# Attention beside a state-space convolution: key bounds moved behind the value transposes, three shift-row buffers, and a redrawn table of 32 stages

## The chip, the cores and the metric

The kernel runs on one core of a Trainium2 chip. Time is the device time of one execution in microseconds (us); for the kernel before it is the median of three runs. TensorE does the matmuls (PE in the profile; PEld is its loading of weights), VectorE is DVE, ScalarE is ACT, GpSimd is POOL and SyncE is SP. SP and POOL issue most of the DMAs. Each engine works through its own instructions in a fixed order; semaphores hold an instruction until what it needs is there.

## The reference

Two independent branches, whose outputs are put side by side:

```python
# A: a diagonal state-space convolution over L = 2048, D = 576, N = 128
K = einsum("dn,dnl,dn->dl", C, exp(dt * A * l), dt * B).real
y = irfft(rfft(pad(K)) * rfft(pad(u)))[:L] + u * Dskip
# B: attention with 32 query heads of 18 columns and one key and value head, S = 2048
q = (x @ wq) split into 32 heads;  k = x @ wk;  v = x @ wv
o = softmax(q @ k.T * 18 ** -0.5) @ v
b = concat(o) @ wo
```

## The kernel before, in words

**Attention** goes through the queries in four chunks of 512 columns, each chunk in 16 pairs of heads, each pair through 16 blocks of 128 keys. One turn for one pair of heads and one key block is called an exponential here, after its largest instruction: two score matmuls (`scores`, line 550, tile s) write a 128x1024 tile in one of three banks of PSUM, ScalarE takes the exponential of it (line 561; line 559 for the first 32, which have a bias) into one of ten P tiles, and TensorE multiplies two such tiles with the values (`product`, line 869, tile ops). There are 1024 exponentials, handled three at a time in `main`. Row 18 of the values is one, so the product also gives the softmax's denominators.

**Fillers** are everything else that TensorE does: query projections (`qproj`, tile q), output projections (`outproj`, tile op), and for the convolution the generation of its kernel (tile kg) and its transforms (hu, lu, hk, lk, iy). They share one bank of PSUM, got by `bank`, and each must be evacuated by VectorE before the next can begin. VectorE also computes the convolution's tables (tab, fr, sum, tt) and its products (acc, pt, us, ks).

**Where the order comes from.** The order of TensorE, VectorE and ScalarE is written out when the kernel is built. A planner, the class `Clock`, holds a planned time of each engine, and `main` puts fillers between scores and products by credits, planned waiting times and constants. `PLAN` sets those constants anew for each stage; a stage is 64 exponentials long (`self.step // 32`, since a step is two exponentials). The functions of the fillers are generators that yield what they wait for: `"v"` and a planned time for VectorE work, `"p"` for TensorE work.

**Key bounds.** The exponential has no running maximum; instead each head gets a bound from the largest absolute values of queries and keys. `settle`, called after the first three exponentials are issued, transposes the values (line 378, tile vp, in the fillers' bank) and copies them to v_sb. `bounds`, called after the third group of three, spreads the keys' maxima by six small matmuls (line 401, tile kmx, also in the fillers' bank) and reduces them to kmax (line 153). No query projection after the first may start before it.

**Shift rows.** After a query projection, `queries` stores its halves qh and ql to a DRAM tile qd through POOL's DMA queue, and `bound` computes the bound of its heads: a small matmul (tile up), a reduction (un), and a row sh (line 145) that POOL's queue writes into qd (line 530). The tile sh has one buffer. SP's queue then fetches the operands (aug) from qd.

**Normalizing.** When the products of a chunk are through, `normalize` loads the denominators, takes their reciprocals, stores them to DRAM (rden), loads them back spread over partitions (db, line 600, two buffers), and multiplies them into the heads' tile oT. The planner lets 4.6 planned us pass from the issue of the load to the multiplication. The output projections of the chunk follow.

**The convolution's sines.** Three times in the loop the convolution needs new powers: ScalarE then loads another table, takes two wide sines (lines 1182, 1184), and loads the table of the exponential again.

**The end.** `finish` divides the last group's products with two reciprocals of 128x256 (lines 701 and 714) and does the partial output projections that are left over (`self.rest`).

Of the kernel before, what the change touches and what calls it, by code (L numbers as in the profile page):

```python
# [9 lines left out]
F32 = mybir.dt.float32  # L10
F16 = mybir.dt.float16
# [6 lines left out]
P = 128  # L18
# [6 lines left out]
CT = 512  # L25
# [17 lines left out]
NS = 3  # L43
# [3 lines left out]
RATE = 1.84  # L47
PACE = 1.79
AHEAD = 0.7
TOTAL = 340.0  # L50
LAST = 576.841

GAP = 0.4
PLAN = {
    0: dict(RATE=1.86, PACE=1.856, AHEAD=0.729, TOTAL=340.0, GAP=0.359, DEFER=0.395, SLACK=3.285, HEAD=17.08, LEFT=1.086, C1=0.549, C2=0.718, C3=0.83, C4=1.39, C5=0.739, C6=1.059, C7=0.572, C8=0.186, C9=0.382, C10=0.431, C11=24.516, C12=11.926),
    1: dict(RATE=1.838, AHEAD=0.731, HEAD=10.76, C3=0.633, C4=1.288, C6=0.962, C8=0.227, C11=22.979),
    2: dict(AHEAD=0.937, TOTAL=426.375, SLACK=2.955, HEAD=8.992, LEFT=1.137, C3=0.83, C4=1.267, C6=0.825, C11=24.516),
    3: dict(AHEAD=0.729, TOTAL=340.0, DEFER=0.389, SLACK=3.285, HEAD=13.454, LEFT=1.086, C2=0.563, C6=1.059, C8=0.186),
    4: dict(PACE=1.877, DEFER=0.395, C2=0.718, C3=0.886, C8=0.257, C12=9.229),
    5: dict(DEFER=0.334, C1=0.507, C3=0.973, C9=0.468, C10=0.418),  # L60
    6: dict(C3=0.912, C4=1.331, C5=0.562, C8=0.216, C9=0.573, C12=11.451),
    7: dict(TOTAL=393.142, HEAD=15.028, C1=0.596),
    8: dict(PACE=1.856, C8=0.186, C12=14.796),
    9: dict(GAP=0.311, DEFER=0.395, C1=0.601, C2=0.561, C6=0.861, C9=0.468),
    10: dict(PACE=1.834, HEAD=14.988, C1=0.497, C9=0.382),
    12: dict(TOTAL=300.519, C1=0.607, C2=0.687, C12=11.271),
    13: dict(AHEAD=0.591, TOTAL=393.142, SLACK=2.63, C1=0.65, C5=0.726, C6=1.059, C10=0.39, C12=14.796),
    14: dict(C1=0.533, C2=0.561, C7=0.595, C9=0.379, C12=11.755),
    15: dict(AHEAD=0.503, C3=1.026, C4=1.582, C8=0.194),
}  # L70
# [143 lines left out]
class Attention:  # L214
# [36 lines left out]
    def setup(self, tp, conv):  # L251
# [5 lines left out]
        nc, cp, a, V = self.nc, self.cp, self.a, self.V  # L257
# [42 lines left out]
        self.outs, self.step, self.due, self.scaled = [], 0, 1 << 30, {}  # L300
        self.o_left = self.q_left = self.units = 0
        self.todo, self.busy, self.group = [], False, 0
        self.tails = []
        self.side_work = Stream(self.side(), self.k, 99.0)
        conv.begin(6)
        p1, small = (self.ps_s.tile([P, 2, CT], F32, tag="s", name=n) for n in ("first", "small"))
# [64 lines left out]
    def settle(self, conv):  # L371

        nc, V, K = self.nc, self.V, self.k
        km, ab, spread = self.km, self.ab0, self.spread
        h2, l2 = self.parts[2:]
        vp = self.bank(CT, "vp").rearrange("p (j n) -> p j n", j=4)
        for j in range(4):
            nc.tensor.transpose(vp[:, j, :], self.vt[:, j * P:(j + 1) * P], self.ident)
        for src, dst in ((ab[96:, 0:1], ab[96:, 1:2]), (km[96:, 4:5], ab[96:, 0:1]), (ab[96:, 1:2], km[96:, 4:5])):
            V.tensor_copy(dst, src)  # L380
        V.tensor_scalar(km[:, 0:4], spread[:, 136:140], km[:, 4:5], None, op0=ALU.mult)
        V.tensor_copy(self.v[:, :, :DH].rearrange("p (c j) d -> p c j d", j=4), vp.rearrange("p j (c d) -> p c j d", c=4)[:, :, :, :DH])
        for m in range(2, 5):
            if m < 4:
                self.place(m, h2, l2, 32 * m - 32, (nc.sync, nc.sync))
            V.memset(self.wq[m][0:1, 0, 0:1], 0.0)
            self.load_wq(m)
        conv.start()
        K.t += 1.0
        K.v = K.t + 2.0  # L390
        K.fill = K.v

    def bounds(self):

        nc, V, K = self.nc, self.V, self.k
        km, spread = self.km, self.spread
        self.bounded = True
        pk = self.bank(20, "kmx")
        for m in range(5):
            for b, n in ((0, 128),) if m < 4 else ((0, 64), (64, 64)):  # L400
                nc.tensor.matmul(pk[b:b + n, 4 * m:4 * m + 4], spread[:, 2 * m:2 * m + n], km[:, 0:4], start=True, stop=True, tile_position=(0, b))
        V.tensor_reduce(self.kmax, pk.rearrange("p (m c) -> p m c", c=4), axis=AX.X, op=ALU.max)
        V.tensor_scalar(self.kmax, self.kmax, FLOOR, 1.002, op0=ALU.max, op1=ALU.mult)
        K.pe(1.5)
        K.v = max(K.v, K.t + 0.5)
        K.fill = K.v + 0.25

    def load_wo(self):
        self.nc.vector.memset(self.wo[0:1, :, 0:1], 0.0)
# [86 lines left out]
    def bound(self, c, m, ab, n0, qd):  # L496

        nc, V, K = self.nc, self.V, self.k
# [73 lines left out]
    def normalize(self, c, ms):  # L572

        nc, V, K = self.nc, self.V, self.k
        od = self.od[c].rearrange("(h r) n -> h r n", r=32)
        if c < NCH - 1:
            oT = self.oT = self.cp.tile([P, 5, CT], F32, tag="oT", name=f"oT{c}")
            o = [oT[:, m, :] for m in range(5)]
        else:
            o = self.heads  # L580
# [13 lines left out]
        tiles, fetched = {}, {}  # L594
# [210 lines left out]
    def main(self, conv, flag):  # L805
        nc, K = self.nc, self.k
# [74 lines left out]
        for r in range(0, len(pairs), NS):  # L881
            new = range(r, min(r + NS, len(pairs)))
            self.step = new[-1] // 2
            globals().update(PLAN.get(self.step // 32, {}))
            ss = {}
            for i in new:
                c, g, kb, j = pairs[i]
                if (g, kb, j) == (0, 0, 0):
                    self.od[c] = self.dr.tile([8 * P, CT], F32, tag="od", name=f"od{c}")
                force(lambda: 16 * c + 2 * g + j in self.ready)  # L890
                ss[i] = self.scores(i, c, 2 * g + j, kb, 0.34 if i == r else 0.216)
            K.t += 0.12
            for i in new:

                while (i - NP) // 2 >= behind:
# [2 lines left out]
                c, g, kb, j = pairs[i]  # L898
# [27 lines left out]
            c, g, kb, j = pairs[new[-1]]  # L926
# [706 lines left out]
```

## Time and profile before

| | us |
|---|---|
| runs | 1140.82, 1141.29, 1143.82 |
| median | 1141.29 |
| the profiled execution's own time | 1140.67 |
| its span | 1138.9 |
| TensorE busy | 1080.4 |
| ScalarE busy | 998.9 |
| VectorE busy | 992.7 |

A row of the timeline has start, duration, engine, line, operation, the tile written, an arrow and the tiles read, and in brackets how long the engine was idle before it and what ended that. A row of waits has who waited for whom, the sum in us, how often, and the longest. A row of a stretch has its ends and length, then the busy time of PE, PEld, DVE, ACT and POOL (instructions in parentheses), the granted clock of TensorE as a share of full speed, the DMAs' share, and GB/s. TensorE's counts are passes: a matmul of 32-bit floats takes two.

### The profile page before, as it was taken

To read this page: it belongs to the slowest core of one execution; us is meant where nothing else is said; L and a number is where in the kernel's file an instruction comes from. 1 tells how busy PE (TensorE), PEld (TensorE's weight loads), DVE (VectorE), ACT (ScalarE), POOL (GpSimd) and SP (SyncE) were. 2 spreads that over 40 slices of the span, in tenths; PEclk is the share of its full clock that TensorE was granted. 3 is DMA by queue.
4 is the path that set the end of the run, shared out by engine and by line. 5 is a ranking of instruction groups with operands and counts; after the bars stand their busy time and mean duration, and the time that the engine had idled before them with its cause. 6 is when DMAs were issued, how large, how long until landed. Compare 5 with 4: busy or idle time off the path is not lost.

```text
span 1138.9 us, 33011 instructions
## 1 busy us (share of the span) xinstructions
PE 1080.4 (95%) x13886; PEld 395.6 (35%) x13886; DVE 992.7 (87%) x1692; ACT 998.9 (88%) x1052; POOL 140.0 (12%) x257
## 2 busy tenths in 40 slices
PE   6999999998998999999999999999989999999997
PEld 2333333333333333323333333333322333433423
DVE  3878998899899898998799899899699799799794
ACT  2878988888997899999898999899999999889993
POOL 4442324122023000000201211000000000000000
PEclk9999999999999999999999999999999999999999
DMA  7432234212222301122202301201222311311201
GB/s 224 146 101 75 64 118 135 63 39 50 84 82 87 95 29 59 50 88 88 89 9 82 106 22 36 97 29 40 68 95 67 99 40 38 97 39 35 72 30 59
DMA packets 59279, 83.37 MB, mean 73 GB/s; under 512 B 14867, under 2 KB 35335, under 8 KB 58613
## 3 DMA queue, kind: packets, MB, share of 16 engines
q1 hardware_dynamic: 47557, 73.24, 20.1%
q0 software_dynamic: 10848, 7.37, 2.6%
q8 instruction: 111, 1.82, 0.7%
q10 hardware_dynamic: 720, 0.58, 0.2%
q14 instruction: 43, 0.35, 0.1%
HBM read 46.59 MB, written 33.85 MB: 71 GB/s over the span
## 4 chain that ended last, share of the span: by engine, by line
PE 59%; DVE 21%; ACT 10%; issue 6%; DMA 3%; POOL 1%; DVEq 0%; SPq 0%; ACTq 0%
PE ops L869 24%; PE s L550 15%; ACT P L561 9%; PE op L211 5%; DVE tab L137 5%; PE kg L1314 3%; DVE ks L137 3%; PE iy L211 3%; PE q L427 2%; DVE acc L137 2%; DVE tt L137 1%; PE hu L211 1%; PE hk L211 1%; DVE pt L137 1%; DMA db<-rden 1%
## 5 line engine op out<-in xcount | busy, mean ns | idle before, releaser
L561 ACT ACTIVATE P<-s 128x1024 f32<-128x1024 f32 x992 | 934.8, 1035 | 97.2 <-PE s L550 94.3
L869 PE MATMUL ops<-P,v_sb 128*32 128x512 f32 x4096 | 509.5, 599 | 3.0 <-DVE o L141 2.8
L550 PE MATMUL s<-aug,kaug 55*128 55x512 f16 x2048 | 307.5, 381 | 23.6 <-ACT P L561 20.8
L550 PEld LDWEIGHTS <-kaug 55*128 55x128 f16 x2048 | 93.2, 94 | 341.6 <-issue 292.9
L869 PEld LDWEIGHTS ops<-P,v_sb 128*32 128x32 f32 x4096 | 118.2, 110 | 162.8 <-issue 131.0
L478 POOL DMA_DIRECT2D qd<-qh x116 | 66.3, 578 | 317.8 <-DVE qh L145 315.2
L427 PE MATMUL q<-x,wq_sb 128*32 128x256 f32 x1360 | 83.6, 382 | 0.3 <-PE s L550 0.3
L211 PE MATMUL op<-wo_sb,oT 126*32 126x288 f32 (+1 forms) x960 | 67.5, 410 | 2.5 <-DVE ob L141 2.5
L1225 POOL MEMSET fr<- 128x192 f32 x24 | 9.9, 497 | 481.6 <-DVE tt L137 242.5
L137 DVE TENSOR_TENSOR tab<-tab,tt 128x576 f32<-128x576 f32 (+1 forms) x72 | 59.0, 820 | 1.5
L137 DVE TENSOR_TENSOR tab<-fr,dif 128x576 f32<-128x576 f32 (+1 forms) x72 | 58.7, 815 | 0.0
L137 DVE TENSOR_TENSOR tt<-fr,sum 128x576 f32<-128x576 f32 (+1 forms) x72 | 58.7, 815 | 0.0
L137 DVE TENSOR_TENSOR tab<-sum,fr 128x576 f32<-128x576 f32 (+1 forms) x72 | 58.6, 814 | 0.0
L137 DVE TENSOR_TENSOR tab<-tab 128x576 f32<-128x576 f32 (+1 forms) x72 | 58.5, 813 | 0.0
L141 DVE COPY ksb<-kg 128x192 f32<-128x192 f32 x48 | 17.3, 360 | 41.5 <-PE kg L1314 41.5
L427 PEld LDWEIGHTS q<-x,wq_sb 128*32 128x32 f32 x1360 | 39.9, 109 | 38.4 <-issue 14.4
L137 DVE TENSOR_TENSOR acc<-acc,pt 128x1728 f32<-128x1728 f32 (+2 forms) x36 | 48.6, 1349 | 0.2
L137 DVE TENSOR_TENSOR pt<-us,ks 128x1728 f32<-128x1728 f32 (+2 forms) x36 | 48.3, 1347 | 0.0
L1314 PE MATMUL kg<-tab 128*32 128x64 f32 x2304 | 41.8, 220 | 5.6 <-DVE tab L137 3.4
L1314 PEld LDWEIGHTS kg<-tab 128*32 128x32 f32 x2304 | 36.5, 110 | 29.6 <-issue 9.8
L559 ACT ACTIVATE P<-s,bias 128x1024 f32<-128x1024 f32 x32 | 33.0, 1115 | 13.4 <-PE s L550 13.4
L137 DVE TENSOR_TENSOR ks<-ks 128x576 f32<-128x576 f32 (+1 forms) x48 | 41.0, 855 | 1.0
(163 smaller groups left out, 1020.9 us busy)
## 6 DMA issues: line engine op xcount, KB each, us to landing
od<-o SPq DMA_DIRECT2D x31, 256.0 KB
aug<-qd SPq DMA_DIRECT2D x124, 55.0 KB
u<-u SPq DMA_DIRECT2D x12, 384.0 KB
kd<-ksb SPq DMA_DIRECT2D x12, 384.0 KB
kt<-kd SPq DMA_DIRECT2D x48, 96.0 KB
outa<-u SPq DMA_DIRECT2D x12, 384.0 KB
pw<-pw SPq DMA_DIRECT2D x8, 528.0 KB
db<-rden SPq DMA_DIRECT2D x16, 252.0 KB
```

What stands on the lines that cost most here:

```text
L137: return self.v.tensor_tensor(out, *a, **k)
L141: return self.v.tensor_copy(out, *a, **k)
L211: nc.tensor.matmul(ps[j:e], w[:, j:e], x, start=start, stop=stop, tile_position=(0, j))
L427: nc.tensor.matmul(ps[o, 256 * f:256 * f + 256], w[:, k, i], xt[:, k, x], start=(k == 0), stop=(k == 4), tile_position=(0, 32 * j))
L478: q.dma_start(qd[h:h + n, row + d:row + d + nd, cs], src[i1:i1 + n * nd, :cs.stop - cs.start])
L550: nc.tensor.matmul(ps[:, j, :], self.kaug[r, kb * P:(kb + 1) * P], t[r, :], start=True, stop=True)
L559: nc.scalar.activation(pt, ps, AF.Exp, bias=self.bias, scale=SCALE / QQ)
L561: nc.scalar.activation(pt, ps, AF.Exp, scale=SCALE / QQ)
L869: nc.tensor.matmul(o_ps[32 * j:32 * j + 32, :], self.v[:, kb, :], pts[2 * n + j // 2][:, j % 2, :], start=(kb == 0), stop=(kb == 15), tile ...
L1225: nc.gpsimd.memset(t[:, :, 0:NF:8], one)
L1314: nc.tensor.matmul(ps[32 * g:32 * g + 32, d, :], t[:, :32], t[:, 32:], start=(j == 0), stop=(j == 1), tile_position=(0, 32 * g))
```

## The change

1. `bounds` is gone as a function of its own. Its matmuls and reductions stand at the end of `settle`, behind the value transposes, and their tile lies in the bank of the heads' products (pool `ps_o`) instead of the fillers' bank.
2. The shift row sh has three buffers instead of one.
3. The planner lets 7.0 planned us pass for the loads of the reciprocals, and 4.6 only after the last scores are issued.
4. `PLAN` has 32 stages of 32 exponentials each, with other numbers in all of them; `LAST` is 728.5 instead of 576.8; the planned cost of the first score tile of three is 0.32 instead of 0.34, and of what follows three 0.10 instead of 0.12.
5. `finish` is not touched.

```diff
-LAST = 576.841
+LAST = 728.54989
...
-    1: dict(RATE=1.838, AHEAD=0.731, HEAD=10.76, C3=0.633, C4=1.288, C6=0.962, C8=0.227, C11=22.979),
+    1: dict(AHEAD=0.72931, TOTAL=288.24614, HEAD=10.10214, C1=0.62524, C6=0.7751, C9=0.37549, C10=0.35145, C11=20.74218),
...
-        self.tails = []
+        self.tails, self.over = [], False
...
         conv.start()
-        K.t += 1.0
-        K.v = K.t + 2.0
-        K.fill = K.v
-
-    def bounds(self):
-
-        nc, V, K = self.nc, self.V, self.k
-        km, spread = self.km, self.spread
         self.bounded = True
-        pk = self.bank(20, "kmx")
+        pk = self.ps_o.tile([P, CT], F32, tag="o", name="kmx")[:, :20]
         for m in range(5):
             for b, n in ((0, 128),) if m < 4 else ((0, 64), (64, 64)):
                 nc.tensor.matmul(pk[b:b + n, 4 * m:4 * m + 4], spread[:, 2 * m:2 * m + n], km[:, 0:4], start=True, stop=True, tile_position=(0, b))
         V.tensor_reduce(self.kmax, pk.rearrange("p (m c) -> p m c", c=4), axis=AX.X, op=ALU.max)
         V.tensor_scalar(self.kmax, self.kmax, FLOOR, 1.002, op0=ALU.max, op1=ALU.mult)
-        K.pe(1.5)
-        K.v = max(K.v, K.t + 0.5)
-        K.fill = K.v + 0.25
+        K.t += 2.3
+        K.fill = K.t - 0.5
+        K.v = K.t + 0.7
...
-        sh = self.p2.tile([8, 256], F16, tag="sh", name=f"sh{c}_{m}", bufs=1)
+        sh = self.p2.tile([8, 256], F16, tag="sh", name=f"sh{c}_{m}", bufs=3)
...
-            yield "v", max(K.t, fetched[m] + 4.6), False
+            yield "v", max(K.t, fetched[m] + (4.6 if self.over else 7.0)), False
...
-            globals().update(PLAN.get(self.step // 32, {}))
+            globals().update(PLAN.get(self.step // 16, {}))
...
-                ss[i] = self.scores(i, c, 2 * g + j, kb, 0.34 if i == r else 0.216)
-            K.t += 0.12
+                ss[i] = self.scores(i, c, 2 * g + j, kb, 0.32 if i == r else 0.216)
+            K.t += 0.1
...
-            if r == 2 * NS:
-                self.bounds()
...
+        self.over = True
```

The first place is TensorE behind the value transposes, at the start of the loop. In the names, s is a score tile, ops the heads' products, kmx the key bounds and q a query projection. Before:

```order
L378 MATMUL vp<-ident,keys 128x128 x4
L550 LDWEIGHTS kaug
L550 MATMUL s_1_1_369<-aug_111,kaug 128x512
...
L550 MATMUL s_1_2_375<-aug_111,kaug 128x512
L869 MATMUL ops_0_394<-P_0_0_307,v_sb 32x512 x2
L869 MATMUL ops_0_394<-P_1_0_309,v_sb 32x512 x2
...
L401 MATMUL kmx<-km,spread_sb 128x4 x4
L401 MATMUL kmx<-km,spread_sb 64x4 x2
L869 MATMUL ops_0_394<-P_0_1_311,v_sb 32x512 x2
...
L427 MATMUL q_1_438<-x_124,wq_sb 32x256 x12
```

And now, at the same place:

```order
L395 MATMUL vp<-ident,keys 128x128 x4
L410 MATMUL kmx<-km,spread_sb 128x4 x4
L410 MATMUL kmx<-km,spread_sb 64x4 x2
L436 MATMUL q_1_379<-x_124,wq_sb 32x256 x16
L559 LDWEIGHTS kaug
L559 MATMUL s_1_1_405<-aug_111,kaug 128x512
...
L559 MATMUL s_1_2_411<-aug_111,kaug 128x512
L436 MATMUL q_1_379<-x_124,wq_sb 32x256 x20
```

The key bounds and the first 16 rows of the query projection now stand ahead of the fourth to sixth score tile, and the first products of the heads come behind all 40 rows of that projection.

The second place is VectorE at the same time; pw and raw are the convolution's powers and coefficients. Before:

```order
L141 COPY v_sb<-vp 128x16x18
L160 MEMSET wq_sb 1x1 x3
...
L137 TENSOR_TENSOR pw_155<-pw_155,m_156 128x528 x2
L137 TENSOR_TENSOR raw_134<-raw_134,dt_130 128x96
...
L153 TENSOR_REDUCE kmax<-kmx 128x5
L145 TENSOR_SCALAR kmax<-kmax 128x5
```

And now:

```order
L158 COPY v_sb<-vp 128x16x18
L177 MEMSET wq_sb 1x1 x3
...
L170 TENSOR_REDUCE kmax<-kmx 128x5
L162 TENSOR_SCALAR kmax<-kmax 128x5
L154 TENSOR_TENSOR pw_155<-pw_155,m_156 128x528 x2
L154 TENSOR_TENSOR raw_134<-raw_134,dt_130 128x96
```

The two reductions of the bounds have moved ahead of the convolution's work.

The third place is VectorE where the first chunk's heads (oT) are multiplied by their reciprocals (db). Before, from the last accumulation behind the reciprocal on (tab and tt are the convolution's tables, pt and acc its products, qh, ql and ab the evacuation of a query projection):

```order
L137 TENSOR_TENSOR pt_2_4421<-us_3843,ks_4040 128x1152
L137 TENSOR_TENSOR tt_0_8_4_4409<-fr_3867,sum_3980 128x576
L137 TENSOR_TENSOR tab_0_4089<-tab_0_4089 128x24x24
L145 TENSOR_SCALAR qh_4_4452<-q_4_4411 128x256
L149 SCALAR_TENSOR_TENSOR ql_4_4453<-q_4_4411,qh_4_4452 128x256
L153 TENSOR_REDUCE ab_4_4454<-qh_4_4452 128x1
L137 TENSOR_TENSOR oT_4254<-oT_4254,db_0_4405 126x512
L137 TENSOR_TENSOR oT_4254<-oT_4254,db_1_4407 126x512
```

And now:

```order
L154 TENSOR_TENSOR tab_0_4019<-tab_0_4019 128x24x24
L154 TENSOR_TENSOR pt_2_4371<-us_3761,ks_3941 128x576
L154 TENSOR_TENSOR tab_0_4019<-tab_0_4019,tt_0_8_4_4356 128x24x24
L154 TENSOR_TENSOR acc_4159<-acc_4159,pt_2_4371 128x96x12
L154 TENSOR_TENSOR acc_4159<-acc_4159,pt_2_4371 128x96x6
L162 TENSOR_SCALAR qh_3_4441<-q_3_4347 128x512
L166 SCALAR_TENSOR_TENSOR ql_3_4442<-q_3_4347,qh_3_4441 128x512
L170 TENSOR_REDUCE ab_3_4443<-qh_3_4441 128x1
L154 TENSOR_TENSOR oT_4187<-oT_4187,db_0_4362 126x512
L154 TENSOR_TENSOR oT_4187<-oT_4187,db_1_4364 126x512
```

The last sum of the table, a product and two accumulations, which stood behind the multiplications, now stand ahead of them, and another query projection is evacuated there.

More of the change, by code (lines that the diff above doesn't have):

```diff
@@ L50 @@
 TOTAL = 340.0
-LAST = 576.841
+LAST = 728.54989
 GAP = 0.4
 PLAN = {
-    0: dict(RATE=1.86, PACE=1.856, AHEAD=0.729, TOTAL=340.0, GAP=0.359, DEFER=0.395, SLACK=3.285, HEAD=17.08, LEFT=1.086, C1=0.549, C2=0.718, C3=0.83, C4=1.39, C5=0.739, C6=1.059, C7=0.572, C8=0.186, C9=0.382, C10=0.431, C11=24.516, C12=11.926),
-    1: dict(RATE=1.838, AHEAD=0.731, HEAD=10.76, C3=0.633, C4=1.288, C6=0.962, C8=0.227, C11=22.979),
[L57 to L69, printed above, removed]
@@ new lines @@
+    0: dict(RATE=1.83766, PACE=1.96256, AHEAD=0.92571, TOTAL=284.66458, GAP=0.37603, DEFER=0.35102, SLACK=3.47335, HEAD=8.62294, LEFT=1.25481, C1=0.54854, C2=0.73058, C3=0.66373, C4=1.29089, C5=0.7692, C6=0.8709, C7=0.57203, C8=0.1836, C9=0.28789, C10=0.38374, C11=17.44673, C12=12.14446),
+    1: dict(AHEAD=0.72931, TOTAL=288.24614, HEAD=10.10214, C1=0.62524, C6=0.7751, C9=0.37549, C10=0.35145, C11=20.74218),
+    2: dict(SLACK=4.50623, C4=1.42363),
+    3: dict(SLACK=3.47335, HEAD=8.62294, C1=0.54854, C4=1.29089, C10=0.46104, C11=23.35201),
@@ new lines @@
+    4: dict(C1=0.42176),
+    5: dict(AHEAD=0.57309, C3=0.61604, C5=0.96612, C8=0.16898, C10=0.34688),
+    6: dict(HEAD=7.28198, C5=0.70322, C9=0.48235),
+    7: dict(HEAD=8.62294, C5=0.96612, C9=0.48686, C10=0.31406),
+    8: dict(LEFT=1.0752, C9=0.37703, C10=0.35755),
+    9: dict(AHEAD=0.62588, C1=0.54854, C3=0.66373, C5=0.7692, C8=0.1836, C10=0.36227, C11=20.74218),
+    10: dict(AHEAD=0.72931, SLACK=3.74107, C1=0.42524, C5=0.99068, C6=0.675, C8=0.14334),
+    11: dict(AHEAD=0.62588, DEFER=0.26061, SLACK=3.47335, C1=0.54854, C2=0.86819, C5=0.7692, C6=0.7751, C8=0.1836, C9=0.29078, C10=0.40013),
@@ new lines @@
+    12: dict(AHEAD=0.72931, GAP=0.38424, DEFER=0.35102, HEAD=9.85705, LEFT=1.25481, C2=0.73058, C4=1.11677, C6=0.7006, C9=0.37549, C10=0.32548),
+    13: dict(AHEAD=0.62588, GAP=0.36205, HEAD=8.62294, C4=1.29089, C6=0.7751, C8=0.21019, C10=0.35145),
+    14: dict(RATE=1.94003, AHEAD=0.47405, C1=0.54366, C7=0.67314),
+    15: dict(GAP=0.47292, HEAD=7.33669, LEFT=1.00362, C9=0.29574, C10=0.30576),
+    16: dict(RATE=2.04977, C2=0.86183, C5=0.95525, C7=0.64327, C11=25.8304),
+    17: dict(HEAD=8.62294, LEFT=1.25481, C1=0.73276, C10=0.41027),
@@ new lines @@
+    18: dict(RATE=1.99267, C1=0.73933, C7=0.54664),
+    19: dict(AHEAD=0.58455, C7=0.68949, C11=32.88172),
+    20: dict(GAP=0.42181, C12=13.78593),
+    21: dict(C6=0.82755, C7=0.59401),
+    22: dict(RATE=1.83766, AHEAD=0.72931, GAP=0.37603, SLACK=2.6878, C1=0.73553, C2=0.83596, C5=0.7692, C6=0.7751, C7=0.57203, C8=0.1836, C9=0.37549, C10=0.35145, C11=20.74218, C12=12.14446),
+    23: dict(GAP=0.45983, C4=1.71673, C5=0.87487, C7=0.65991, C11=27.90351),
+    24: dict(RATE=1.958, GAP=0.37603, SLACK=3.47335, C1=0.60115, C2=0.73058, C4=1.57705, C5=0.7692, C7=0.73314, C10=0.43243, C11=20.74218),
@@ new lines @@
+    25: dict(RATE=1.83766, GAP=0.45983, SLACK=2.6878, C1=0.73553, C2=0.83596, C3=0.60936, C4=1.71673, C5=1.2212, C7=0.64158, C8=0.14483, C10=0.35705, C11=27.90351),
+    26: dict(SLACK=2.29415, LEFT=0.89109, C3=0.66373, C4=1.94285, C5=0.87487, C7=0.65991, C8=0.1836, C10=0.35145),
+    27: dict(GAP=0.37603, SLACK=3.47335, LEFT=1.25481, C1=0.72441, C2=0.73058, C4=1.29089, C5=0.7692, C7=0.57203, C8=0.22911, C11=20.74218),
+    28: dict(DEFER=0.44331, SLACK=2.52932, C1=0.6663, C4=1.27923, C5=0.96193, C7=0.65524, C8=0.27768, C10=0.43231),
@@ new lines @@
+    29: dict(AHEAD=0.80461, TOTAL=332.67272, GAP=0.38313, DEFER=0.40584, C3=0.79933, C4=1.29089, C5=0.7692, C7=0.82973, C8=0.22911),
+    30: dict(AHEAD=0.72931, TOTAL=288.24614, GAP=0.37603, DEFER=0.35102, SLACK=4.77729, C1=0.54854, C3=0.66373, C7=0.57676, C8=0.1836, C9=0.32463, C10=0.35145, C11=26.29615, C12=11.67446),
+    31: dict(RATE=1.78096, AHEAD=0.80461, TOTAL=332.67272, GAP=0.38313, DEFER=0.40584, SLACK=2.52932, C1=0.6663, C3=0.79933, C7=0.82973, C8=0.22911, C9=0.37549, C10=0.43231, C11=20.74218, C12=12.14446),
```

## The prediction

> **What bounds the kernel now.** I read the page's busy line first, then the busy time in three stretches, then who waited for whom on TensorE and VectorE, and last the timeline around each long wait.
>
> ```profile
> span 1138.9 us, 33011 instructions
> PE 1080.4 (95%) x13886; PEld 395.6 (35%) x13886; DVE 992.7 (87%) x1692; ACT 998.9 (88%) x1052; POOL 140.0 (12%) x257
> 0.00:26.00 26.00, 17.11 (x154) 5.12 (x154) 8.15 (x21) 6.60 (x8) 10.93 (x24) 1.00 0.81 241
> 26.00:1123.00 1097.00, 1053.56 (x13608) 386.10 (x13608) 976.53 (x1658) 991.58 (x1042) 129.05 (x234) 1.00 0.22 69
> 1123.00:1139.00 16.00, 9.74 (x136) 4.38 (x128) 8.00 (x14) 0.77 (x2) 0.00 (x0) 0.91 0.23 78
> ```
>
> The main loop runs from 26 to 1123 us, and in it TensorE is busy for 1053.6 of 1097 us. The change leaves the loop's matmuls alike but for eight, so it can win only what TensorE loses between them: 43.4 us of idle time, plus the stretches in which it ran at half clock. Who makes TensorE and VectorE wait:
>
> ```profile
> PE s L550 <- ACT P L561: 20.8, 76, 0.5
> PE up L211 <- DVE ql L149: 3.8, 3, 2.2
> PE kg L1314 <- DVE tab L137: 3.4, 4, 2.6
> PE kg L1314 <- DVE un L153: 2.2, 1, 2.2
> DVE sh L145 <- DMA qd<-sh: 4.7, 3, 2.1
> DVE kmax L153 <- PE kmx L401: 3.8, 1, 3.8
> DVE oT L137 <- DMA db<-rden: 3.1, 3, 1.4
> ```
>
> Almost half of it (20.8 us) is score matmuls that wait for ScalarE, in 76 pieces of at most 0.5 us; that is the price of stretches without filler work. The rest is a few long waits for VectorE, behind which stand three waits of VectorE's own: the shift rows, the key bounds, and the rows of reciprocals.
>
> **Head: key bounds behind the value transposes.** Before:
>
> ```profile
> 28.95 0.39 PE L550 MATMUL s<-aug,kaug 55*128 55x512 f16 x2 [0.56 <-ACT P L559]
> 29.96 0.51 PE L550 MATMUL s<-aug,kaug 55*128 55x512 f16 x2 [0.61 <-ACT P L559]
> 32.27 1.42 PE L550 MATMUL s<-aug,kaug 55*128 55x512 f16 x6
> 33.62 1.27 PE L401 MATMUL kmx<-km,spread_sb 128*128 128x4 f32 x12
> 37.11 0.82 PE L550 MATMUL s<-aug,kaug 55*128 55x512 f16 x6
> 30.40:33.80 3.40, 3.40 (x18) 0.77 (x16) 0.68 (x5) 3.40 (x4) 3.40 (x7) 0.54 0.46 112
> ```
>
> Two score tiles waited 0.56 and 0.61 us for an exponential to free their bank. Directly afterwards the granted clock was 0.54 over 3.4 us, and six score matmuls took 1.42 us where they take 0.82 at full clock. Now the six key-bound matmuls (1.27 us, the same ones) and 16 rows of the first query projection stand between the transposes and those score tiles, so the banks are free by the time the scores come up: −1.17 us. The half clock cost 0.60 us on these scores alone, and at most 3.4 × 0.46 = 1.6 us in all; I put it at 1.3. Whether it goes depends on more than two gaps, so I take half, −0.65. VectorE now reduces the bounds ahead of the convolution's power products. The matmuls follow the transposes at once, so it waits at most their 1.27 us where it waited 3.8. Behind that wait stand the convolution's tables and the evacuation of the first query projection, and these come at least 2.5 us sooner; that covers TensorE, which comes sooner by less. The first product of the heads must wait until the borrowed bank is read, but it stands 40 query rows later. Ends: +1.3 (the new VectorE wait is passed on) and −2.5 (gaps and half clock in full). Taken: −1.8.
>
> **Three buffers for the shift rows.** With one buffer, the next shift row waits until the DMA has read the last one:
>
> ```profile
> 78.05 0.28 DVE L145 TENSOR_SCALAR sh<-u 8x256 f16<-8x256 f32 x1 [2.06 <-DMA qd<-sh]
> 89.71 0.88 PE L1314 MATMUL kg<-tab 128*32 128x64 f32 x48 [2.19 <-DVE un L153]
> 269.94 0.28 DVE L145 TENSOR_SCALAR sh<-u 8x256 f16<-8x256 f32 x1 [2.06 <-DMA qd<-sh]
> ```
>
> From 78.05 to 89.5 VectorE works without a break, and TensorE waits 2.19 us for the end of it. The order of both engines is the same in the new kernel there, so the 2.06 us come through nearly whole: −2.0. What is late next is the kernel generation itself, with 0.1 us left. At 270 us no long TensorE wait follows, and the order around it is redrawn: between 0 and −2.06, taken −0.6, nearer to the first since VectorE is 87% busy but not the bound. The third (0.6 us of the 4.7) lies in the next part. POOL issues the same DMAs.
>
> **The reciprocal rows are waited for 7.0 instead of 4.6 planned us.** This is one number in the diff, and it moves VectorE's multiplications behind other work:
>
> ```profile
> 334.37 1.56 SPq L600 DMA_DIRECT2D db<-rden  x2
> 340.84 0.69 DVE L137 TENSOR_TENSOR oT<-oT,db 126x512 f32<-126x512 f32 x1 [1.42 <-DMA db<-rden]
> 342.69 0.69 DVE L137 TENSOR_TENSOR oT<-oT,db 126x512 f32<-126x512 f32 x1 [1.16 <-DMA db<-rden]
> 344.09 0.74 DVE L137 TENSOR_TENSOR pt<-us,ks 128x576 f32<-128x576 f32 x1
> 345.43 2.13 DVE L137 TENSOR_TENSOR acc<-acc,pt 128x1152 f32<-128x1152 f32 x2
> 345.64 0.88 PE L1314 MATMUL kg<-tab 128*32 128x64 f32 x48 [2.59 <-DVE tab L137]
> 347.88 0.50 PE L211 MATMUL up<-sel_sb,aw 128*32 128x8 f32 x24 [0.61 <-DVE ksb L141]
> 348.23 3.24 PE L869 MATMUL ops<-P,v_sb 128*32 128x512 f32 x16
> 347.80:351.20 3.40, 3.32 (x40) 0.92 (x40) 2.83 (x8) 2.00 (x3) 0.81 (x2) 0.54 0.32 87
> 352.85 1.90 PE L869 MATMUL ops<-P,v_sb 128*32 128x512 f32 x16
> ```
>
> The two rows were issued from 334.37 on and used 6.5 us later; VectorE stood still for 1.42 and 1.16 us, with the last table products queued behind, and TensorE waited 2.59 us for these and 0.61 us more behind them. Then the clock fell to 0.54 and sixteen passes of the product took 3.24 instead of 1.90 us. In the new order the table is finished ahead of the multiplications, and four more large VectorE steps stand between reciprocal and multiplication: a 576-wide product (0.74 us), a table sum of the same width, and the two accumulations (2.13), 3.6 us of cover against 2.58 us of wait. So both waits and their followers go: −3.2; of the 1.34 us of half clock I again take half, −0.65. Ends: 0 (another late table takes the place) and −4.5. The output projections start later; that is part of the next count. In two later chunks the multiplications also move back, but VectorE lost only 0.5 us there. Taken: −3.85.
>
> A rule speaks against my halves of the half clock. The Trainium skill ("TensorE: Matmul & The Clock Gate", section "HAM oscillation — how this bites in real kernels") says that the clock is cut by TensorE-idle gaps above about 3.4 us. By it gaps of 2.6 us have nothing to do with it, and the sum would be 1.3 us higher. This trace disagrees: the three cuts inside the loop came right behind the gaps of 1.2 (in two), 2.19 and 2.59 us.
>
> ```profile
> 134.65 0.22 PE L211 MATMUL up<-sel_sb,aw 128*32 128x8 f32 x5 [2.19 <-DVE ql L149]
> 136.20:139.60 3.40, 3.40 (x20) 0.65 (x17) 3.37 (x6) 2.85 (x3) 3.40 (x7) 0.54 0.32 82
> ```
>
> This one stays: TensorE's order ahead of it (one query projection in one piece, one product, then the bound that needs its evacuated tile) is the same in both kernels.
>
> **The table.** From about the 160th exponential on, filler work (query and output projections, transforms, kernel generation) stands at other places. Its price is what ScalarE makes TensorE wait where filler is missing:
>
> ```profile
> 830.14 36.40 ACT L561 ACTIVATE P<-s 128x1024 f32<-128x1024 f32 x39
> 851.76 0.39 PE L550 MATMUL s<-aug,kaug 55*128 55x512 f16 x2 [0.20 <-ACT P L561]
> 852.68 0.39 PE L550 MATMUL s<-aug,kaug 55*128 55x512 f16 x2 [0.52 <-ACT P L561]
> 478.79 2.63 PE L211 MATMUL op<-wo_sb,oT 126*32 126x288 f32 x40
> 829.23 1.66 PE L211 MATMUL op<-wo_sb,oT 126*32 126x288 f32 x24 [1.74 <-DVE ob L141]
> ```
>
> At 0.93 us an exponential, TensorE loses 0.20 + 0.52 us on every six, 0.12 us each. Stretches of twelve or more exponentials without filler hold 141 exponentials before (the longest 42) and 114 now (the longest 33), so 27 × 0.12 = −3.2 us. Against that stands ScalarE's second excursion to the convolution's sines, where 20 of 40 rows of output projection have moved out of the 16 exponentials around it: one such bank is 2.63 us. Net −0.6, with −3.2 and +2.6 as near ends. Banks are handed over closely (under 1 us of other work) 80 times before and 78 times now, so I expect as many late handovers as before: 0.
>
> **The end.** The reciprocals stay. Two partial output projections more are left over for it, which are missing in the loop:
>
> ```profile
> 1120.71 0.67 PE L211 MATMUL op<-wo_sb,wq_sb 126*32 126x288 f32 x8
> 1128.37 0.30 PEld L715 LDWEIGHTS bc<-rc_last,b 128*128 128x128 f32 x2 [0.53 <-DVE rc_last L714]
> ```
>
> Each is some 0.49 us of issue (0.67 less a drain of about 0.18). One fits into the 0.53 us wait for the second reciprocal, the other lengthens the end: −0.98 + 0.49 = −0.5.
>
> **Sum.** −1.8 − 2.6 − 3.85 − 0.6 − 0.5 = −9.35. The profiled execution took 1140.67 us, so 1131.3; the median of the runs before is 0.6 us above it, 1141.29, which gives 1131.9, rounded 1132.
>
> **The rivals.**
> 1. *Handed back.* The redrawn order has as many new late handovers as the old places that go (0.6 + 2.0 + 3.2 + 1.17 + 0.6 = 7.6 us by the sum), so that only the end and the two halves of the clock stay won: −1.8, 1139.5. For it: all the redrawn stages lie behind the head, and an in-order VectorE makes such waits wherever the plan is off. Against it: two of the waits are cured by a buffer and by cover, not by luck. 0.20.
> 2. *The clock is cut anyway,* as that rule would have it, at moments of its own: without the two halves 1133.3. 0.10.
> 3. *Filler counts in full.* The whole −3.2 of the stretches and both half clocks: −2.5 − 2.6 − 4.5 − 3.2 − 0.5 = −13.3, 1128.0. 0.15.
> 4. *Slower: output projections that start later starve the second sine excursion and its followers.* The place is around the 400th to the 416th exponential, with ScalarE away at its sines. TensorE then lacks one bank of 2.6 us; a gap of that size has been followed by half clock (1.3 us more), and each of the three handovers around it may wait for a late copy, which at 827 us cost 1.74 us. That is 2.6 + 1.3 + 3 × 1.74 = 9.1. It decides from a cost of 9.4 + 3.4 = 12.8 on, so two such places are needed (each of the three excursions offers one), or one and the failure of the head and shift-row gains. At two: 1141.3 − 9.4 + 18.2 = 1150; at one with those gains lost, 1141.3 − 5.0 + 9.1 = 1145.4. Taken: 1146. 0.12.
>
> That the change does not do what it says is excluded by the order for the buffers and the head, which stand as told.
>
> **Numbers.** My case has 0.43. A difference of 0.3% (3.4 us) is about what a measurement of this kernel can tell from none: faster is below 1137.9, slower above 1144.7. Faster: 0.43 + 0.10 + 0.15 = 0.68; same: 0.20; slower: 0.12. The range, 1125 to 1142, leaves out rival 4.
>
> **What would show it.** VectorE's waits for the shift rows and for the reciprocal rows vanish from the list of waits, and its wait for the key bounds is about 0.9 us. The wait of kernel generation near 88 us falls from 2.19 to about 0.1, and no gap of over 2 us stands near 340 us. The clock shows a cut near 135 us and at most one other in the loop. TensorE's idle time in the loop falls from 43 to some 35 us, and its wait for ScalarE stays near 20 us. I am wrong if the listed waits go and as many others of over 1 us appear, or if the score matmuls wait for ScalarE by several us more.

## The result and the profile after

The changed kernel took 1124.54 us (median of 4 runs, 1122.69 to 1125.14) against 1141.05 us (4 runs, 1140.0 to 1143.82) of the kernel before on the same chip: a ratio of 0.9856 (95% interval 0.984 to 0.9872), or 16.5 us less. The forecast was 1132, with 1125 as the lower end of its range, so the time fell by 7 us more than the sum held. The profiled execution took 1125.13 us.

The page's first lines, and who waited for whom on TensorE and on VectorE, of the changed kernel:

```profile
span 1123.4 us, 32998 instructions
PE 1075.3 (96%) x13886; PEld 395.7 (35%) x13886; DVE 992.7 (88%) x1690; ACT 998.2 (89%) x1052; POOL 141.0 (13%) x257
...
PE s L559 <- ACT P L570: 20.8, 77, 0.5
PE op L228 <- DVE ob L158: 2.5, 2, 1.6
PE up L228 <- DVE ql L166: 2.3, 1, 2.3
PE lu L228 <- DVE scu L158: 1.1, 1, 1.1
PE ops L878 <- DVE o L158: 0.8, 3, 0.3
PE kg L1322 <- DVE un L170: 0.2, 1, 0.2
...
DVE kmax L170 <- PE kmx L410: 0.9, 1, 0.9
```

TensorE is busy for 5.1 us less, with the same matmuls. Some 4.3 us of that, by an estimate, is half clock that it no longer has: the span holds 4.5 us of it instead of 13.1, and matmuls take about twice as long there (eight passes of the product 1.94 us instead of 1.04, in rows below). The other 10.4 us of the span are idle time. The waits of VectorE for the shift rows (4.7 us) and for the reciprocals' rows (3.1 us) are gone from the list, the one for the key bounds is 0.9 us, and what ScalarE costs is 20.8 us as before.

The head of the loop, and the table's matmuls that had waited 2.19 us at 89.71 us, in the timeline of the changed kernel:

```profile
27.77 1.14 PE L410 MATMUL kmx<-km,spread_sb 128*128 128x4 f32 x11
28.83 1.93 PE L436 MATMUL q<-x,wq_sb 128*32 128x256 f32 x32
30.70 0.82 PE L559 MATMUL s<-aug,kaug 55*128 55x512 f16 x6
31.45 2.37 PE L436 MATMUL q<-x,wq_sb 128*32 128x256 f32 x40
...
84.12 0.88 PE L1322 MATMUL kg<-tab 128*32 128x64 f32 x48 [0.16 <-DVE un L170]
```

No score matmul waits there, the six scores take 0.82 us (full clock), and the generation of the convolution's kernel waits 0.16 us. The one wait of over 2 us that is left stands where the prediction had left it; the second fence is the row of the stretch behind it, with the granted clock in the third place from the end:

```profile
125.70 1.04 PE L878 MATMUL ops<-P,v_sb 128*32 128x512 f32 x8
129.05 0.29 PE L228 MATMUL up<-sel_sb,aw 128*32 128x8 f32 x8 [2.31 <-DVE ql L166]
129.15 1.94 PE L878 MATMUL ops<-P,v_sb 128*32 128x512 f32 x8
```

```profile
129.00:132.40 3.40, 3.35 (x22) 0.50 0.23 55
```

It is the only stretch at half clock inside the loop; the kernel before had three. TensorE's busy time in five stretches of the loop, of the kernel before:

```profile
26.00:210.00 184.00, 175.34 (x2388) 0.98 0.35 106
210.00:420.00 210.00, 199.14 (x2594) 0.99 0.21 64
420.00:620.00 200.00, 191.40 (x2474) 1.00 0.21 67
620.00:860.00 240.00, 230.77 (x2902) 1.00 0.19 62
860.00:1107.00 247.00, 240.90 (x3080) 1.00 0.18 59
```

and of the changed kernel:

```profile
26.00:210.00 184.00, 178.10 (x2442) 0.99 0.35 106
210.00:420.00 210.00, 204.95 (x2716) 1.00 0.21 64
420.00:620.00 200.00, 194.85 (x2552) 1.00 0.23 73
620.00:860.00 240.00, 227.56 (x2842) 1.00 0.19 61
860.00:1107.00 247.00, 242.18 (x3064) 1.00 0.17 55
```

Length less busy time is idle time. It fell by 2.8 us in the first stretch, 5.8 in the second, 3.5 in the third and 1.3 in the last, and rose by 3.2 in the fourth. The second stretch alone holds more than the sum had given to everything behind 210 us (0.6 + 3.2 + 0.6). (The stretches are cut by time; the changed kernel, which is up to 15 us ahead, has somewhat later work in each.) So the question of the experiments is whose those microseconds are: the buffers', the due time's, or the table's.

### The profile page after: what moved, and what is told of

Same layout as the page of the kernel before. It is cut to its first block, busy times and chain, and to the rows that moved or that the text cites. A ratio compares the mean times of both kernels' runs of the same rounds, so it can differ in the third digit from the quotient of the medians.

```text
span 1123.4 us, 32998 instructions
## 1 busy us (share of the span) xinstructions
PE 1075.3 (96%) x13886; PEld 395.7 (35%) x13886; DVE 992.7 (88%) x1690; ACT 998.2 (89%) x1052; POOL 141.0 (13%) x257
## 4 chain that ended last, share of the span: by engine, by line
PE 67%; DVE 13%; ACT 13%; issue 5%; DMA 1%; DVEq 0%; ACTq 0%
PE ops L878 28%; PE s L559 18%; ACT P L570 12%; PE op L228 6%; PE q L436 3%; PE iy L228 3%; DVE tab L154 3%; PE kg L1322 3%; DVE ks L154 2%; PE hk L228 1%; PE lu L228 1%; DVE acc L154 1%; PE hu L228 1%; PE lk L228 1%; DVE pt L154 1%
## 5 line engine op out<-in xcount | busy, mean ns | idle before, releaser
L559 PE MATMUL s<-aug,kaug 55*128 55x512 f16 x2048 | 306.3, 381 | 23.7 <-ACT P L570 20.8
L436 PEld LDWEIGHTS q<-x,wq_sb 128*32 128x32 f32 x1360 | 39.5, 109 | 39.7 <-issue 16.5
```

Source lines behind the costliest of these rows:

```text
L436: nc.tensor.matmul(ps[o, 256 * f:256 * f + 256], w[:, k, i], xt[:, k, x], start=(k == 0), stop=(k == 4), tile_position=(0, 32 * j))
L559: nc.tensor.matmul(ps[:, j, :], self.kaug[r, kb * P:(kb + 1) * P], t[r, :], start=True, stop=True)
```

## The experiments

Each was timed against the kernel before on its chip; 0.001 of a ratio is 1.14 us. Line numbers in the rows are those of each run's own kernel. Where it says that the order is held, the planner was kept from noticing the edit, so that every other instruction stands where it stood.

### The local parts alone

**Three shift-row buffers in the kernel before.**

```diff
-        sh = self.p2.tile([8, 256], F16, tag="sh", name=f"sh{c}_{m}", bufs=1)
+        sh = self.p2.tile([8, 256], F16, tag="sh", name=f"sh{c}_{m}", bufs=3)
```

> The kernel before with three sh buffers and nothing else; the order of every engine is that of before. Theory L (each edit is worth the gap it closes on TensorE, and no more): the wait of sh for its buffer goes, the gaps near 88 and 270 us close, -2.6 us, so 1138.0 to 1139.0 against 1141.1. Rival B (the buffers free VectorE's queue along the whole loop, and the 6 us that the sum lacked are theirs): -5 us or more, 1136 or below, with gaps gone elsewhere too. Rival T (what the sum lacked is the redrawn order): the same as L here.

Measured 0.9967 (0.995 to 0.9985), −3.8 us, between the two theories; the interval holds L's −2.6 and also B's −5. In the trace L's places are right. A longer stretch at half clock in the head (10.24 us instead of 3.41) sets the kernel back by 2.8 us; behind it 2.0 us are won ahead of the 64th exponential and 1.2 near 270 us. Another 1.3 come around the half clock near 345 us, and next to nothing more to the end.

**The key bounds behind the value transposes in the kernel before,** the six matmuls (the expectation's twenty are their columns) and two reductions moved to the end of `settle`, order held.

> The kernel before with the twenty key-bound matmuls and their two VectorE steps moved behind the value transposes, into the heads' bank; the planner is held, so that the order of everything else is that of before. Theory L: -1.8 us by the sum on record, -2.6 by the start of the 32nd exponential in the changed kernel's trace, so 1138.5 to 1139.3; the first half-clock stretch near 30 us gone. Rival B: no more than L, -1 us or so. Rival T: as L. If it gives nothing, the head's gain was taken back later in the loop and belongs to the sum's 'handed back' rival.

Measured 0.9982 (0.9967 to 0.9998), −2.1 us: L. The expectation failed in one point: the half clock near 30 us stayed (it began at 29.7 us). The 32nd exponential started 2.5 us sooner, but the first one already started 0.6 sooner, before anything that the edit touches: 1.9 us are the edit's. Then 1.6 went again ahead of the 64th, behind a stretch at half clock at 87.7 us that the profile of before doesn't have.

**One shift-row buffer in the changed kernel,** order held.

> The changed kernel with one sh buffer again; its order is not touched. Theory L: the waits return in part, since other places now stand beside them: +1.5 to +2.9 us, 1126 to 1127.5 against 1124.5. Rival B: +5 us or more, 1129.5 or above. Rival T: +1 to +3, as the table was fitted with three buffers and another order meets the same DMA waits elsewhere.

Measured 0.9887 (0.986 to 0.9914), +3.5 us against the changed kernel's 0.9856, with an interval of about as much. The profile says what the interval can't: the wait comes back, 2.2 us of it at one place, and the exponentials from the 64th on all start 2.2 to 2.4 us later.

```profile
DVE sh L162 <- DMA qd<-sh: 2.8, 2, 2.2
```

So theory B falls: the buffers are worth their own waits.

**Both in the kernel before,** order held.

> The kernel before with three sh buffers and the key bounds behind the value transposes, the planner held: the old order stands but for these. If the two local gains add: 0.9967 and 0.9982 give 0.9949, 1135 to 1136 against 1141. If they take from the same slack: 0.9965 to 0.998. If the pair is worth more together: 0.992 or less.

Measured 0.9945 (0.9929 to 0.9962), −6.3 us: they add. Counted from the first exponential, its 160th starts 5.1 us sooner than before's, the changed kernel's 5.8: nearly all that the change wins up to there is these two edits. Behind that the two win another 1.4 us near 270 us and next to nothing more.

### The table and the due time

**The new table alone** (`PLAN` of 32 stages, `LAST`; bounds, buffer, 4.6 and the small costs as before).

> The kernel before with the new table of 32 stages and its LAST and nothing else (bounds at their old place, one sh buffer, 4.6 us for the reciprocal's rows). Theory L: -0.6 us plus or minus 2 by the sum on record, 1138.5 to 1142.5. Rival T (the redrawn order alone carries what the sum lacked, by handing over fewer steps late): -5 to -9 us, 1132 to 1136. Rival F (the table only fits together with the later due time of the reciprocal rows, and hands over as late as before without it): 0 to +6, 1141 to 1147.

Measured 1.0171 (1.0142 to 1.0201): 19.5 us slower than before, worse than any theory allowed. Two gaps of 4.4 and 4.7 us stand around ScalarE's third excursion to the sines, and each is followed by half clock (6.83 and 3.41 us).

```profile
855.46 1.92 PE L886 MATMUL ops<-P,v_sb 128*32 128x512 f32 x16
861.81 0.61 PE L567 MATMUL s<-aug,kaug 55*128 55x512 f16 x2 [4.43 <-ACT P L578]
...
879.21 1.94 PE L886 MATMUL ops<-P,v_sb 128*32 128x512 f32 x8 [4.69 <-DVE o L158]
```

**7.0 alone in the kernel before.**

```diff
-            yield "v", max(K.t, fetched[m] + 4.6), False
+            yield "v", max(K.t, fetched[m] + (7.0 if self.todo is not None and self.step < 511 else 4.6)), False
```

> The kernel before with 7.0 instead of 4.6 us as the planner's due time of the reciprocal's rows, and nothing else: old table, old head, one sh buffer. The order changes from the first normalization on. Theory L: the waits for the db rows go and the gaps of 2.59, 0.90 and 0.79 us behind them, -3.85 us by the sum on record, 1136 to 1138. Theory I (the parts of the order belong together: table, bank's length, due times; any one alone is worse or no better than before, all together are better than their sum; the new table alone, 19.5 us slower, is its first witness): 0 to +8 us although the db waits go, with other late handovers in their place.

Measured 1.0087 (1.0069 to 1.0106), 10 us slower. The waits for the reciprocals' rows do go from VectorE's list, as L says, but the redrawn order meets the single shift-row buffer in their place, and TensorE waits 3.61 us for the copies queued behind it:

```profile
354.85 0.28 DVE L145 TENSOR_SCALAR sh<-u 8x256 f16<-8x256 f32 x1 [5.67 <-DMA qd<-sh]
...
356.32 1.07 PE L427 MATMUL q<-x,wq_sb 128*32 128x256 f32 x16 [1.66 <-DVE ksb L141]
361.01 1.93 PE L869 MATMUL ops<-P,v_sb 128*32 128x512 f32 x8 [3.61 <-DVE o L141]
```

**4.6 in the changed kernel.**

> The changed kernel with 4.6 us again as the due time of the reciprocal's rows. Theory L: the db waits return, +3.85 us plus or minus 2, 1126.5 to 1130.5 where the changed kernel has 1124.5. Theory I: the new table is only good beside 7.0: +8 us or more, 1132 or above, the TensorE gaps spread over many places and not only behind the db rows.

Measured 0.9901 (0.9885 to 0.9918): +5.1 us, in L's range. But L's reason fails. VectorE waits only 0.4 us for the rows (second line), and the gap of 2.59 us near 345 us, which the sum had given to the due time, does not come back: the stretch from 210 to 420 us is as busy as in the changed kernel (204.67 and 204.95). The time is lost later, at the copies of the heads' products (tile o), which now stand in VectorE's queue behind the convolution's work:

```profile
PE ops L878 <- DVE o L158: 4.6, 7, 1.7
...
DVE oT L154 <- DMA db<-rden: 0.4, 1, 0.4
...
210.00:420.00 210.00, 204.67 (x2680) 1.00 0.21 64
420.00:620.00 200.00, 192.42 (x2508) 1.00 0.23 72
```

**The old table in the changed kernel,** everything else new.

> The changed kernel with the old table of 16 stages and its LAST: head, three sh buffers, 7.0 and the small costs stay. By the sum on record the table is worth 0.6 us, so Theory L: 1124.5 to 1126.5 plus 0.6, that is 1124 to 1128. With the table carrying what the sum lacked, +5 to +7: 1129 to 1132. Theory I: the old table beside the new parts is worse than before itself had it: 1135 to 1145.

Measured 0.9998 (0.9983 to 1.0013): 16 us slower than the changed kernel, all that the change had won. Theory I.

**The new table and 7.0, with the old head and one buffer.**

> The kernel before with the new table and 7.0, but the bounds at their old place and one sh buffer. The new table alone stood at 1.0171 of before. Theory L: 7.0 takes only the db waits from that, -4 us, 1150 to 1157. Theory I, with the due time as the missing partner: most of the 19.5 us comes back, 1127 to 1134. Theory I with the head's order as the missing partner (the planner's clock is set otherwise after the head, and every later step is shifted): it stays at 1145 or more.

Measured 1.0115 (1.0097 to 1.0133), some 1154 us, which both L and the theory with the head as the partner allow: 7.0 takes 6.4 us from the table's 19.5, and the rest stays. So 7.0 is not the partner that makes the new table good. The head, the buffers and the small costs are more of it: with these and 4.6 the table stood at 0.9901. The suspicion was that it fits one course of the planner alone.

### Redrawing the order by nothing

A cost in the planner that is 5 or 10 ns larger changes nothing that the chip does but the order. `main` adds 0.12 planned us after each three scores in the kernel before, 0.1 in the changed one.

```diff
-            K.t += 0.12
+            K.t += 0.125
```

> The kernel before with the same 5 ns (0.125 for 0.12), and nothing else. Theory I: its old table fits its own course as well, and a redrawn one is worse: 1146 to 1160 against 1141. Theory P: 1139 to 1143.

> The kernel before with 0.13 for 0.12: a second redrawn order with none of the edits. Both theories: 1.010 to 1.020, 1152 to 1164. Under 1.005 it would say that 0.125 was an unlucky draw and that the old table isn't fitted to one course.

Measured 1.0144 (1.011 to 1.0177) and, with 0.13, 1.0149 (1.0118 to 1.018): both some 17 us slower than before. So the old order, too, is better than those beside it, and the first nudge shows what it had avoided. TensorE's wait list has one entry of 9.9 us; VectorE's timeline shows why:

```profile
PE ops L869 <- DVE o L141: 16.2, 6, 9.9
...
863.35 3.66 DVE L137 TENSOR_TENSOR stage<-stage,m 128x792 f32<-128x792 f32 x4 [3.21 <-ACT stage L1182]
...
872.14 0.68 DVE L141 COPY o<-ops 128x512 f32<-128x512 f32 x1
```

The products' copy stands behind the sines' work on VectorE, which itself waits for ScalarE; the next group's products wait for the copy. The sines start 36 us later than in before, whose row stands first here:

```profile
825.79 1.62 ACT L1182 ACTIVATE stage<-stage,hp_sb 128x1584 f32<-128x1584 f32 x1
861.70 1.61 ACT L1182 ACTIVATE stage<-stage,hp_sb 128x1584 f32<-128x1584 f32 x1
```

This one place carries most of the loss. In before the third sines follow the 738th exponential, in both nudged kernels the 771st. Between the 704th and the 800th TensorE then idles 16.2 and 16.1 us instead of 7.4, and 10.24 us at half clock follow, by an estimate 13.9 us in all (8.8 us more of idle time and half of 10.24); the two profiled executions are 13.3 and 16.2 us longer. In three other slow orders (the new table alone or with 7.0, and the old costs below) they follow the 759th, and TensorE idles 16.3, 11.5 and 12.8 us there. The slow orders that have them at the 732nd, as the changed kernel has (7.0 alone, the old table, 0.105), lose elsewhere. No run moved the sines alone.

> The changed kernel with one of the planner's costs 5 ns larger in each round of scores (0.105 for 0.1); nothing that the chip does is changed but the order, which is redrawn over the whole loop. Theory I (the table's numbers fit one course of the planner's clock, step by step, and say nothing beside it; a redrawn order lands 5 to 20 us higher, whatever it was redrawn by): 1130 to 1145 against 1124.5. Theory P (the earlier bad mixtures lacked one certain partner, the head or the due time, and the table is good wherever these stand): 1123 to 1127.

> The changed kernel with 0.095 for 0.1; a smaller part of the order moves than with 0.105. Theory W: as 0.105, 0.992 to 1.002 (the redrawn orders with the edits keep 14 to 20 us under those without). Theory F (a better fit, not worth more edits): 1.000 to 1.010. At 0.986 to 0.988 the table would bear this nudge.

> The changed kernel with the old costs of a round of scores (0.34 and 0.12 for 0.32 and 0.1), the one part of the change that the runs of the new table alone had left old. Theory I: one more redrawn order, 1130 to 1145. Theory P with these costs as the missing partner: 1140 to 1155, as bad as the new table alone. If neither holds, 1123 to 1127.

In the changed kernel 0.105 for 0.1 gives 0.9948 (0.9928 to 0.9968), 10.5 us slower; 0.095 gives 0.9862 (0.9835 to 0.9889), no difference; the old costs (0.34 and 0.12) give 1.0025 (1.0008 to 1.0042), 19 us slower. But 0.095 redraws next to nothing: of some 1100 groups of equal TensorE instructions in the traces, all but 8 stand in the same sequence as in the changed kernel, where 0.105 moves some 280 and the old costs 350. So the new order, too, is better than those beside it, and the nudge that was borne is no evidence against it. Theory P falls with the other two.

**The two local edits in the nudged kernel before,** order held against 0.125.

> The same two edits in the nudged kernel before (0.125), whose order is held but for them; the nudged kernel stood at 1.0144. Theory F (the refit: each edit is worth its local gaps in any order, some 6 us, and the rest of the 16.5 us is that the new table fits its course better than the old one did): 1.0144 less 0.005, so 1.008 to 1.0105. Theory W (the edits are worth more where the order was not fitted around their waits; redrawn orders with them stood 9 to 10 us under those without): 1.003 to 1.007.

Measured 1.0108 (1.0082 to 1.0133) against 1.0144 without them: −4.1 us, just outside F's figure and far from W's. The local edits measure 4 to 6 us in a good order and in a bad one, each figure known to a few us.

### The wait that is left

The first bound of the second chunk is handed to TensorE behind the next product (first run), or behind the next two (second; the third is the second on the order of 0.095). Order held elsewhere.

```diff
+        if (c, m) == (1, 0):
...
+            self.held = rest
+        else:
+            rest()
```

> The changed kernel with the first chunk's-end bound matmuls up1_0 handed to TensorE behind the four products that follow them (their rows on VectorE and GpSimd with them), the planner held: the order elsewhere is that of the changed kernel. In the changed kernel TensorE waits 2.31 us for them at 126.74 us, and the half-clock stretch of 3.41 us comes at 129.0. The products' exponentials were done by 121.0 us, so the gap shrinks to 0.3 to 0.6: -1.8 us, and -1.5 more if the half clock goes with it: 1121 to 1122.8 against 1124.5. If the four products wait for something else, or ScalarE sets the pace there, 1124 to 1125.

> The changed kernel with up1_0 behind the next two products and the three pairs of scores between them, the planner held. In e12, behind one product, a gap of 1.46 us was left and the half-clock stretch went. Behind two the rows on VectorE should be done before TensorE asks: the gap of 2.31 us goes wholly, and no window of 3.41 us near 126 us idles for half its length: -2.3 from the gap and some -1 from the clock on the mean of the runs, 1121 to 1122.5, ratio 0.9835 to 0.9855. If the time saved there is only waited out at the next scores (TensorE waits for ScalarE's exponentials behind its table load), 1123.5 to 1124.5, 0.9855 to 0.987.

> The same on the order with 0.095 for 0.1, which stood at 0.9862. If its order is as good as the changed kernel's: as e17, 0.983 to 0.9855; the pair of e17 and e18 on the same chip tells whether the two orders differ at all.

Measured 0.9862 (0.983 to 0.9895), 0.9876 (0.9855 to 0.9898) and 0.9874 (0.9853 to 0.9895): no gain over the changed kernel's 0.9856 that these intervals could tell. In the profiles the half clock is gone and the time from the first to the last exponential is 1.1 to 1.5 us shorter. Even that is not the edit's: the kernel with 0.095 and the bound in its old place, which still waits 2.32 us there, also shows no half clock, and its loop is within 0.4 us of these three. The gap is not won: in the second run TensorE gets past the bound and waits for ScalarE, which is back from its sines only then.

```profile
127.67 0.39 PE L573 MATMUL s<-aug,kaug 55*128 55x512 f16 x2 [1.00 <-ACT P L584]
128.58 0.39 PE L573 MATMUL s<-aug,kaug 55*128 55x512 f16 x2 [0.52 <-ACT P L584]
129.50 0.39 PE L573 MATMUL s<-aug,kaug 55*128 55x512 f16 x2 [0.53 <-ACT P L584]
```

That is the mechanism of its expectation's second branch, at a ratio just above the range given there. The third run was expected at 0.9855 at most and lies above it, though its interval reaches it. No version was found that beats the changed kernel.

## Why the prediction was wrong

A chain of measured kernels leads from before to after, one part at a time: 1 → 0.9945 (head and buffers) → 0.9901 (table, small costs and the planner's clock after the head) → 0.9856 (7.0). Each link is known to 2 to 3 us. Added in another order the parts would share it out otherwise: alone in the kernel before, 7.0 cost 10 us and the table 19.5.

| part | sum on record | measured |
|---|---|---|
| head and buffers | −1.8 − 2.6 = −4.4 | −6.3 |
| table | −0.6 | −5.0 |
| 7.0 | −3.85 | −5.1 |
| end | −0.5 | in the table's link |
| all | −9.35 | −16.5 |

**Head and buffers: right as told, within what the runs can tell.** VectorE's waits go. Counted from the first exponential, the 32nd starts 1.9 us sooner in the trace of the head alone, 2.1 in that of both edits and 2.2 in the changed kernel, where the sum had 1.8. That this is so near is partly luck: in the trace of both edits score tiles still wait 0.19, 0.30 and 0.61 us in the head, nearly the 1.17 that were to go, and the half clock, of which the sum took half, stayed in the trace of the head alone at about the same gain. The shift rows gave 2.0 up to the 64th, as forecast, and 1.4 near 270 us where the sum had 0.6. One more microsecond of that profile is a cut near 135 us that didn't come. The interval of the measured 6.3 us, 4.3 to 8.1, just holds the sum's 4.4.

**7.0: the size near by luck, the place wrong.** "So both waits and their followers go: −3.2": they go, but with the new table they are gone at 4.6 as well. The 5.1 us of the due time lie from 420 us on; most of them are copies of the products that no longer queue behind other work (4.6 us of waits with 4.6, 0.8 with 7.0).

**The table is the step that failed:** "Banks are handed over closely (under 1 us of other work) 80 times before and 78 times now, so I expect as many late handovers as before: 0." The 0 was the mis-sized term. A count of close handovers does not say how late each is; that depends on what VectorE has in its queue just then. The table's other term did not show either: 27 fewer exponentials without filler were to save 3.2 us of TensorE's waits for ScalarE, and these are 20.8 us before and after. Idle time in the stretch from 210 to 420 us, with head and buffers alone and order held, was still

```profile
210.00:420.00 210.00, 200.53 (x2598) 0.99 0.22 66
```

9.5 us, and 5.3 with the new table at 4.6: −4.2 us, among them the 2.59 us near 345. And the redrawn orders with the same edits (0.105, the old costs, the old table) idle 8 to 14 us more than the changed kernel. Redrawing an order of this kernel by small costs of the planner cost 10 to 19 us each time that it moved more than a few instructions, and the change swaps one good order for a better one, by some 5 us. The table's numbers have no worth of their own: the same table stood in a kernel 16.5 us faster than before and in one 19.5 us slower. Why exactly the new order is the better by 5 us stays open beyond the waits named; where the third sines stand can be read from an order, but the two good orders have them at nearly the same place.

**The end:** from the start of the last score tile to the end of the span it was 19.4 us before and 19.2 now: −0.2, not −0.5, and less than the 0.7 us by which it differs among the four profiles with before's order.

**The half clock, taken by half, was too timid.** Two of three stretches went in the profile, which is one draw. Over the 90 runs of the kernel before that the experiments brought, time and mean granted clock go together (correlation −0.85, 0.87 us for each 0.001). Their mean clock was 0.9949, that of the changed kernel's four runs 0.998, which by that slope makes 2.7 us where the sum had 1.3. The measured figures above hold this already.

**The rivals.** The third, filler in full (1128.0), was nearest, but for another reason: ScalarE's share stayed at 20.8 us, and the gain came from VectorE's. The first, handed back, is refuted for this order, and true of the old table beside the new parts (0.9998). The fourth has its mechanism in the nudged kernels before, at the third excursion, but with a copy stuck in VectorE's queue and 9.9 us instead of a missing filler bank and 2.6; in the changed kernel it does not occur. Every point of "what would show it" came out: the waits gone, 0.9 us for the key bounds, 0.16 at the kernel generation, the one cut at 129 us, idle time in the loop from 43.4 to 33.4 us. These signs all belong to the local waits, so they could not tell that the table's term was wrong.

## What to carry to other kernels

In a kernel whose order is drawn by a planner, an edit has two prices: the wait that it takes away, which a trace shows to 1 or 2 us and which adds up, and the order that it redraws, which was worth 10 to 19 us here and which the count of handovers in before's trace did not foresee. Hold the order to measure the first, and nudge a planner's constant by nothing to learn the size of the second (after a look at whether the nudge moves the order at all), before any number of the sum is believed. Where the constants are refitted with the edit, forecast the local sum and widen the range on both sides by that size.

## What the runs showed of the hardware

**The clock is cut by windows.** The clock records of all 20 profiles come in pieces that are multiples of 3.413 us, but for the last piece of each, which the end cuts off (17.07, 102.40 and 208.21 us of full clock in the kernel before are 5, 30 and 61), and a cut lasts one such window or more. Laid on that grid, behind the first 45 us and up to the last 20 us, of the windows at full clock that TensorE idled for 1.75 us or more, 30 of 30 were followed by a window at half clock; of those with 1.5 to 1.75 us, 3 of 16; of those with less, none of about 6200. (In the last 20 us, 2 of 4 with 1.75 us or more.) A gap near 2.2 us is thus cut or not by where the grid's border falls in it. In the kernel before the gap of 2.19 us ahead of 89.71 us lies across a border, 0.6 us in one window and 1.6 in the next. That next window and the one behind it ran at full clock (third place from the end):

```profile
88.10:91.50 3.40, 1.79 (x74) 1.00 0.59 144
91.50:94.90 3.40, 3.40 (x91) 1.00 0.35 130
```

The other gap of 2.19 us, ahead of 134.65, lay in one window and was cut. The last long wait of the changed kernel shows the same: 2.31 us in one window were cut, and with 0.095 the 2.32 us at the same place, 1.05 in one window and 1.27 in the next, were not. The grid's place differs from run to run, which may be why the same kernel's runs differ by up to 10 us; that was only argued. In the first 45 us cuts also came behind windows with 0.4 to 1.4 us of idle time, and what cuts there stays open. So in the loop no gap of the length that the prediction weighed is needed: about half a window, 1.7 us, inside one window is enough.

**A gap that is closed can be waited out at the next engine.** Behind ScalarE's sines the 2.31 us of the last long wait turned into 1.00 + 0.52 + 0.53 us for ScalarE when the bound was taken out of the way.
